# Planned decode-attention and gated-MLP backward: keys load first, layer norm by batch statistics, output weights contiguous per partition, order found anew

## The chip, the core and the metric

The kernel runs on one core of a Trainium2 chip. The metric is the device time of one execution in microseconds (us). The core has a matrix engine (TensorE, PE in the profile; its weight loads are PEld), VectorE (DVE), ScalarE (ACT), GpSimd (POOL) and SyncE (SP), which here issues transfers. Transfers between the device memory and the on-chip buffer run on 16 DMA engines.

## The reference

One step of a decoder block with its backward pass. Two rows (batch 2, one token each, 576 wide) go through a layer norm; its result feeds an attention over cached keys and values and a gated MLP without a nonlinearity, side by side:

```python
xn = _layernorm(x)                                   # (2, 1, 576), eps 1e-5
q = (xn @ wq)                                        # 32 heads of 128, 16 key heads
p = softmax(q . k * 128 ** -0.5)                     # over 4096 cached keys
a = (p @ v) @ wo                                     # wo: (4096, 576)
h = (xn @ w_gate) * (xn @ w_up)                      # 4608 wide
out = x + a + h @ w_down
```

The kernel returns `out` and the gradients, for a given `grad_out`, of x, the key and value caches, wq, wo, w_gate, w_up and w_down. All are bf16. Each cache is 33.5 MB and is read once; its gradient, of the same size, is written once. So all inputs are read and gradients of the same size are written: 92.5 MB each way.

## The kernel before

The work is cut into eight groups of two key heads (`NG`), each with two batch rows, so 16 steps (`NS`, index s; group s // 2). A step loads four 1 MB blocks (two keys, two values) into the shared buffers `big` (16 of them; `CAP`, line 298, caps how many serve as loaded blocks `kv`, transposed blocks `X`, stores being filled `st`, and gate and up blocks `G`). Per step:
- `turn` transposes each block in 32x32 tiles on DVE (L457), two instructions of 128x1024 per block.
- `softmax` and `dscore` (PE L1162) compute scores and score gradients, with small steps on DVE (L1224 the maximum, L1279, L1290) and ACT (mr, ex, pr); the results are `pp` and `dd`.
- `head_outer` (PE L1183) writes the cache gradients: the block-diagonal `BD` (built on POOL, L1150) times `pp` gives out_3 (values), times `dd` gives out_2 (keys). Each 1 MB store is evicted from PSUM in four casts of 128x1024 on ACT (L461) or DVE (L463).
- `contract` (PE L1335) gives the attention output (t = 1) and the gradient of q (t = 0), held in `oT`.

Per group, `group_front` computes q (PE L908), spreads it (`rep`, event Eq), then transposes wo (DVE L457), multiplies it with `Wdy` (PE L941) and turns the result into the second half of `qd` through `dof` (DVE L457, ACT L950); the event is Ed. `group_back` takes `oT` to `R` by PE transposes (L969) and makes out_5 (rows, casts of 128x576), out_4 (columns, casts of 128x1024; its tail in `tl`), and the sums `acc` (L987) and `accx` (L1012) for out_0 and out_1.

The MLP runs in nine blocks of 512 columns (`mlp`), loaded in pairs: gate and up (1 MB each, `G`, with their last 64 rows in `gu`) and two w_down blocks (`ww`). It writes out_8 (rows), out_6 and out_7 (columns, 1 MB per pair, complete only when both halves are done).

`front` (L564 on) loads x and grad_out by ACT's queue, computes the layer norm in five passes on ACT (L574 to L582), transposes it to `xs` (event Exn) and copies grad_out and the normed rows to all partitions (`dyr`, `xnr`, L608), and grad_out in columns to `Wdy` (event Edy). Its intermediates lie in buffers of `st`. `consts` builds selector tiles on DVE; `clears` zeroes ten tiles on POOL.

The order of everything is planned when the program is built. Each piece is a generator (a stream) that yields requests: an engine for a time, a buffer (ACQ, REL), an event (WAIT, SET), a transfer, or a priority (PRIO). `Order.run` keeps a model of each engine's and the transfer queue's time and always lets the request go on that can start first; among requests for one engine within `SLACK` of it the lowest priority number wins. Priorities come from `pr(name, s)`: a base `PR`, edges `HEAD` and `TAIL`, and an offset per step `OFF`, numbers found by a search outside the program. `EV(cols)` picks ACT or DVE for an eviction by their planned times and `BIAS`. `WQ_AT`, `WO_AT` and `MLP_AT` gate when weight loads may be issued, counted in key and value blocks already issued. What comes out is a fixed instruction order per engine; each engine runs it strictly in order. SP's order holds all loads (L1044 caches, L1059 to L1068 wq and wo, L1083 to L1092 MLP) and all stores (L681), so a store that waits for its evictions holds up every load behind it.

## Time and profile before

| | |
|---|---|
| median of 3 runs | 483.37 us (482.95 to 486.26) |
| the profiled execution, its own time | 483.47 us |
| its span, first to last instruction | 481.7 us |
| moved by DMA, mean rate | 185.94 MB, 386 GB/s |
| q1, the queue of nearly all transfers, share of 16 engines | 98.0% |
| busy: PE / DVE / ACT / POOL | 80% / 75% / 71% / 32% |
| mean granted TensorE clock | 0.675 |
| out_dram<-big stores of 1 MB | 72, 12.2 us to landing |
| key / value loads of 1 MB | 32, 11.5 us / 32, 13.1 us |
| wo loads of 576 KB | 8, 12.3 us |

The profile is one execution. Its slices give, for forty equal parts of the span, the busy tenths of each engine, the granted TensorE clock and what the DMA engines moved. A table of stretches gives the same for chosen times, with busy microseconds and counts. The DMA share is time of packets over 16 engines; packets overlap, so a full queue reads 1.00 to 1.08. The queue of an issuing engine (SPq) shows when each issue ran: an issue that waits starts late or is long, and what is merged in one line (x7) is a row of issues.

### The profile page before, as it was taken

The page shows a single profiled execution, that of the slowest core. Times are in us where ns is not written, and L with a number is a line of the kernel's source. Part 1 is how long each engine was busy: PE and PEld are TensorE (multiplying, and loading weights), DVE is VectorE, ACT ScalarE, POOL GpSimd, SP SyncE. Part 2 cuts the span into 40 slices and gives each one's busy share as a digit, 9 for nine tenths or more (in the row PEclk, how much of TensorE's full clock was granted, in tenths as well). Part 3 has the DMA queues.
Part 4 walks back from the last instruction along what each step waited for, and adds up shares of the span by engine and source line. Part 5 has one row for each costly group of instructions (what it writes and reads, how often), then busy time and mean ns, then how long its engine had stood idle before and what let it go on. Part 6 is the DMA issues. An engine that isn't in the chain of part 4 may idle for free.

```text
span 481.7 us, 15312 instructions
## 1 busy us (share of the span) xinstructions
PE 386.8 (80%) x6530; PEld 217.9 (45%) x6530; DVE 360.0 (75%) x667; ACT 343.2 (71%) x520; POOL 155.4 (32%) x220
## 2 busy tenths in 40 slices
PE   1479699858788878868977899857698899899897
PEld 1456345435444444434654345324465434554444
DVE  8688877867377977776677778866665988788872
ACT  6066578956787596755598779856578877868883
POOL 3110553443011374320026364361102724074100
PEclk9995657669656578677786557756965555765765
DMA  7997999999999999999999999999999999999994
GB/s 289 353 406 269 367 387 386 401 343 399 424 406 417 390 416 420 365 399 407 415 406 417 342 407 422 424 403 388 413 386 411 420 326 403 419 395 419 405 412 163
DMA packets 49652, 185.94 MB, mean 386 GB/s; under 512 B 4008, under 2 KB 21168, under 8 KB 33200
## 3 DMA queue, kind: packets, MB, share of 16 engines
q1 hardware_dynamic: 49576, 184.96, 98.0%
q8 instruction: 51, 0.84, 0.7%
q14 instruction: 17, 0.14, 0.1%
q10 hardware_dynamic: 8, 0.00, 0.0%
HBM read 92.48 MB, written 92.48 MB: 384 GB/s over the span
## 4 chain that ended last, share of the span: by engine, by line
DMA 46%; PE 30%; ACT 10%; DVE 7%; issue 4%; SPq 3%; DVEq 0%; ACTq 0%
DMA out_dram<-big 29%; ACT big L461 8%; PE ps_o L1183 6%; PE ps_m L1335 5%; DMA big<-in_A_k_cache_dram 5%; DMA big<-in_A_v_cache_dram 5%; PE ps_m L1162 4%; DVE big L457 3%; DMA ww<-in_B_w_down_dram 3%; PE ps_o L715 3%; DMA ww<-in_A_wo_dram 2%; PE ps_m L941 2%; DVE big L463 2%; DMA ww<-in_A_wq_dram 1%; PE ps_o L701 1%
## 5 line engine op out<-in xcount | busy, mean ns | idle before, releaser
L461 ACT CAST big<-ps_o 128x1024 bf16<-128x1024 f32 (+1 forms) x319 | 283.0, 955 | 41.0 <-PE ps_o L1183 22.1
L457 DVE STREAM_TRANSPOSE big<-big 128x1024 f32<-128x1024 f32 x146 | 175.8, 1223 | 23.9 <-DMA out_dram<-big 17.0
L1150 POOL TENSOR_TENSOR BD<-vr,mask 128x2048 bf16<-128x2048 bf16 x32 | 115.3, 3602 | 114.1 <-PE ps_o L1183 40.8
L463 DVE CAST big<-ps_o 128x1024 bf16<-128x1024 f32 (+1 forms) x57 | 66.4, 1166 | 12.8 <-PE ps_o L1183 4.3
L1162 PE MATMUL ps_m<-big,W 128*32 128x128 bf16 x2048 | 60.4, 286 | 4.2 <-POOL W L1127 1.3
L1162 PEld LDWEIGHTS <-W 128*32 128x32 bf16 x2048 | 47.8, 127 | 22.4 <-issue 19.3
L1183 PE MATMUL ps_o<-BD,dd 32*128 32x512 bf16 x256 | 51.4, 527 | 7.5 <-ACT big L461 5.5
L1183 PE MATMUL ps_o<-BD,pp 32*128 32x512 bf16 x256 | 47.6, 520 | 8.4 <-ACT big L461 6.4
L1127 POOL COPY W<-rep 32x16 bf16<-32x16 bf16 x128 | 24.5, 192 | 69.9 <-DVE rep L925 65.0
L661 POOL COPY wt<-wm 64x128 bf16<-64x128 bf16 (+1 forms) x34 | 8.9, 261 | 99.2 <-DVE wm L654 98.3
L457 DVE STREAM_TRANSPOSE big<-ww 128x1152 f32<-128x1152 f32 x25 | 34.1, 1365 | 7.5 <-DMA out_dram<-big 4.8
L1335 PE MATMUL ps_m<-big,dd 128*32 128x512 bf16 x256 | 28.8, 540 | 9.8 <-DVE dd L457 4.7
L1335 PE MATMUL ps_m<-big,pp 128*32 128x512 bf16 x256 | 30.2, 566 | 1.4 <-DVE pp L457 0.9
L1183 PEld LDWEIGHTS <-dd 32*128 32x128 bf16 x256 | 12.0, 98 | 30.6 <-issue 26.5
L1183 PEld LDWEIGHTS <-pp 32*128 32x128 bf16 x256 | 11.0, 98 | 24.7 <-issue 21.1
L701 PEld LDWEIGHTS <-xnr 32*128 32x128 bf16 x416 | 13.7, 110 | 14.4 <-issue 12.9
L715 PE MATMUL ps_o<-dyr,R 32*32 32x288 bf16 x256 | 18.1, 396 | 2.1 <-ACT big L461 1.1
L461 ACT CAST osb<-ps_m 128x512 bf16<-128x512 f32 x16 | 9.6, 598 | 12.7 <-PE ps_m L1335 9.3
L941 PE MATMUL ps_m<-big,Wdy 128*128 128x128 bf16 x144 | 15.4, 292 | 3.4 <-DVE cr L1287 1.8
L701 PE MATMUL ps_o<-hb,xnr 32*128 32x128 bf16 x288 | 14.3, 250 | 4.5 <-ACT big L461 3.2
L715 PE MATMUL ps_o<-dyr,hb 32*32 32x288 bf16 x288 | 16.1, 337 | 1.1 <-DVE tl L463 0.5
L941 PEld LDWEIGHTS <-Wdy 128*128 128x128 bf16 x144 | 13.8, 134 | 6.3 <-issue 6.3
(198 smaller groups left out, 486.6 us busy)
## 6 DMA issues: line engine op xcount, KB each, us to landing
out_dram<-big SPq DMA_DIRECT2D x72, 1024.0 KB, 12.2
big<-in_A_k_cache_dram SPq DMA_DIRECT2D x32, 1024.0 KB, 11.5
big<-in_A_v_cache_dram SPq DMA_DIRECT2D x32, 1024.0 KB, 13.1
out_dram<-big SPq DMA_DIRECT2D x17, 576.0 KB, 10.8
ww<-in_B_w_down_dram SPq DMA_DIRECT2D x9, 576.0 KB, 12.4
out_dram<-big SPq DMA_DIRECT2D x10, 512.0 KB, 9.6
ww<-in_A_wo_dram SPq DMA_DIRECT2D x8, 576.0 KB, 12.3
ww<-in_A_wq_dram SPq DMA_DIRECT2D x8, 512.0 KB, 9.7
```

Source lines behind the costliest of these rows:

```text
L457: nc.vector.transpose(out, in_)
L461: nc.scalar.copy(out, in_)
L463: nc.vector.tensor_copy(out=out, in_=in_)
L661: nc.gpsimd.tensor_copy(view(Wt[:], 64 * h, 64, 0, [[dims[-1][1], n], [1, dims[-1][1]]]), view(Wm[:], 64 * h, 64, off, dims))
L701: nc.tensor.matmul(o[:, aa, dc * P:(dc + 1) * P], lhsT=xnr[32 * a:32 * a + 32, dc * P:(dc + 1) * P], rhs=rhs(a), start=True, stop=True)
L715: nc.tensor.matmul(o[32 * q:32 * q + 32, aa, 0:HD2], lhsT=view(t, 32 * q, 32, 2 * A + aa, [[4, 32]]), rhs=dyr[32 * q:32 * q + 32, k * HD2: ...
L941: nc.tensor.matmul(dp, lhsT=Wdy[:, e, 2 * k:2 * k + P], rhs=view(X[:], 0, P, 64 * k + e, [[D, GH], [2, 32]]), start=(k == 0 and e == 0), s ...
L1127: nc.gpsimd.tensor_copy(view(W_t[t][w][:], 32 * a, 32, 6 + 8 * a, [[G * WW, 4], [WW, G], [1, 2]]), view(rep_t[grp[g]["qs"]][:], 32 * a, 32 ...
L1150: nc.gpsimd.tensor_tensor(BD_t[i][:], view(vr_t[v][:], 0, P, 0, [[0, 16], [1, Dh]]), view(mask16[:], 0, P, 0, [[1, 16], [0, Dh]]), ALU.mult)
L1162: nc.tensor.matmul(sc[32 * cq:32 * cq + 32, :], lhsT=view(W[:], 0, P, (be * G + l) * WW + 6 - 4 * c2 - 2 * l, [[1, 32]]), rhs=view(X[:], 0 ...
L1183: nc.tensor.matmul(o[:, k, :], lhsT=pr2[32 * c4:32 * c4 + 32, :], rhs=BD[32 * c4:32 * c4 + 32, 8 * l + 4 * h2:8 * l + 4 * h2 + 4, :], star ...
L1335: nc.tensor.matmul(ct[32 * j:32 * j + 32, :], lhsT=view(rT, 0, P, 4 * c + 2 * l, [[1, 32]]), rhs=kv_t[kvS[s][t][l]][:, Dh * c:Dh * (c + 4) ...
```

## The change

The layer norm takes mean and variance from VectorE's batch statistics (`bn_stats`, `bn_aggr`), then one square root on ACT and one subtract-and-multiply on DVE; ACT loads its square-root table before the rows arrive. The grad_out rows get a stream of their own (`front_y`), and the intermediates tiles of their own, so the `st` buffers are free from the start; a new event Exr stands for the normed rows on all partitions. The first key block is issued ahead of all else on SP. All clears run on DVE before the other constants. wo is loaded with four consecutive rows per partition (4608 bytes) instead of four rows 128 apart; to match, `dof` is taken through a PE transpose, and the output product reads `rT`, a transpose of `R`. A group's tail piece alternates between the halves of its buffer. The first step's key `BD` waits for Eq alone. CAP lets X hold 9 buffers instead of 12. All numbers of the search (OFF, HEAD, TAIL, PR and those shown) are new.

In the built order SP issues: the first key block, wq, wo, gate and up of the first pair with their tails, both w_down blocks, one key, two value, two key and one value block, then the first stores (out_8, two tails, out_8, out_6, out_7, two tails), then a value and a key block. Before, it was: wq, two key blocks, one value block, wo, gate and up, both w_down blocks, one value, two key and one value block, then out_8, two tails, a value and a key block, out_6, out_7. At the end, the last MLP block's loads follow the last value block; before, three key and value blocks followed them.

```diff
--- before.py
+++ after.py
-CAP = {"kv": 7, "X": 12, "st": 4, "G": 2}
...
-MLP_AT = [2.38, 3.44, 16.76, 17.06, 29.05, 44.32, 47.73, 43.88, 59.6]
-WQ_AT = [-3, 9, 17, 23, 32, 39, 50, 55]
-WO_AT = [2, 7, 5, 25, 36, 39, 37, 57]
+CAP = {"kv": 7, "X": 9, "st": 4, "G": 2}
...
+MLP_AT = [0, 6.72, 15.68, 13.64, 27.33, 41.52, 44.61, 38.32, 79.54]
+WQ_AT = [-2, 8, 17, 24, 34, 38, 50, 44]
+WO_AT = [-14, 7, 0, 22, 36, 40, 42, 56]
...
-LM, LAG = 0.15, 1.75
+LM, LAG = 0.61, 1.67
...
-BIAS = 0.547
-SLACK = {"PE": 0.08, "ACT": 0.3, "DVE": 0.46, "POOL": 24.94, "SP": 1554.58}
+BIAS = 0.347
+SLACK = {"PE": 0.04, "ACT": 0.27, "DVE": 0.49, "POOL": 11442.77, "SP": 11922.52}
...
-    dof = const.tile([P, GH, 32], FP32, name="dof")
+    dof = const.tile([P, P], BF16, name="dof")
+    rT = const.tile([P, GH, 32], BF16, name="rT")
...
-    var = const.tile([2, 1], FP32, name="var")
...
-    xs = filled("xs", [P, 6, 32], BF16, 0.0, nc.gpsimd)
-    Wdy = filled("Wdy", [P, 2, 160], BF16, 0.0, nc.gpsimd)
+    xs = filled("xs", [P, 6, 32], BF16, 0.0)
+    Wdy = filled("Wdy", [P, 2, 160], BF16, 0.0)
...
+    for t in (*W_t[0], *W_t[1], *wm_t, *wt_t, *oT_t):
+        nc.vector.memset(t[:], 0.0)
...
-    Exn, Edy, Econst, Ezero = Event(), Event(), Event(), Event()
+    Exn, Exr, Edy, Econst, Ezero = Event(), Event(), Event(), Event(), Event()
...
-        for t in (*W_t[0], *W_t[1], *wm_t, *wt_t, *oT_t):
-            yield POOL(0.37)
-            nc.gpsimd.memset(t[:], 0.0)
...
-    def carve(t, n):
-        return pairs(t[:])[0:2, D * n:D * (n + 1)]
-
...
+    xnb = const.tile([2, D], BF16, name="xnb")
+    bst = const.tile([2, 2, 6], FP32, name="bst")
+    mv = const.tile([2, 2], FP32, name="mv")
+
+    def widen(src, dst):
+        i = yield ACQ("o")
+        o = o_t[i]
+        yield PE(0.24)
+        for k in range(2):
+            nc.tensor.matmul(o[:, k, 0:HD2], lhsT=sel2[:].rearrange("b a m -> b (a m)"),
+                             rhs=src[:, k * HD2:(k + 1) * HD2], start=True, stop=True)
+        e = yield EV(D)
+        cp(e, dst[:].rearrange("p (k n) -> p k n", k=2), o[:, :, 0:HD2])
+        yield REL("o", i)
+
+    def front_y():
+        yield WAIT(Ein)
+        yield from widen(xy[:, D:2 * D], dyr)
+        dyT = xnr[:].rearrange("p (k m) -> p k m", m=32)
+        yield DVE(0.8)
+        t32(xnr[:], view(dyr[:], 0, P, 0, [[64, NB], [1, 2], [2, 32]]))
+        yield DVE(0.8)
+        for a in range(4):
+            nc.vector.tensor_copy(
+                view(Wdy[:], 32 * a, 32, 32 * a, [[2, NB], [160, 2], [1, 2]]),
+                dyT[32 * a:32 * a + 32, :, 0:2].rearrange("p (k e) b -> p k e b", e=2))
+        yield SET(Edy)
...
-        x_f, xc = carve(st_t[1], 0), carve(st_t[1], 1)
-        xnb = st_t[2][0:2, 0:D]
+        yield SPAWN(front_y(), -999.0)
+        yield ACT(1.5)
+        nc.scalar.activation(warm[:], eps_t[0:1], AF.Sqrt)
...
-        yield ACT(4.0)
-        nc.scalar.activation(x_f, xb, AF.Copy, accum_out=nmu[:])
-        nc.scalar.activation(nmu[:], nmu[:], AF.Copy, scale=-1.0 / D)
-        nc.scalar.activation(xc, x_f, AF.Identity, bias=nmu[:], scale=1.0)
-        nc.scalar.activation(x_f, xc, AF.Square, accum_out=var[:])
-        nc.scalar.activation(rstd[:], var[:], AF.Sqrt, bias=eps_t[:], scale=1.0 / D)
-        yield DVE(0.15)
+        yield DVE(1.0)
+        for k in range(2):
+            nc.vector.bn_stats(bst[:, k], xb[:, k * HD2:(k + 1) * HD2])
+        nc.vector.bn_aggr(mv[:], bst[:].rearrange("p k s -> p (k s)"))
+        yield ACT(0.3)
+        nc.scalar.activation(rstd[:], mv[:, 1:2], AF.Sqrt, bias=eps_t[:], scale=1.0)
+        yield DVE(0.6)
...
-        yield ACT(0.8)
-        nc.scalar.activation(xnb, xc, AF.Copy, scale=rstd[:])
-        yield ACT(1.7)
+        nc.vector.tensor_scalar(xnb[:], xb, mv[:, 0:1], rstd[:], op0=ALU.subtract, op1=ALU.mult)
+        yield ACT(1.5)
...
-        yield DVE(0.5)
+        yield DVE(0.4)
...
-
-        for src, dst in ((yb, dyr), (xnb, xnr)):
-            i = yield ACQ("o")
-            o = o_t[i]
-            yield PE(0.24)
-            for k in range(2):
-                nc.tensor.matmul(o[:, k, 0:HD2], lhsT=sel2[:].rearrange("b a m -> b (a m)"),
-                                 rhs=src[:, k * HD2:(k + 1) * HD2], start=True, stop=True)
-            yield DVE(0.75)
-            nc.vector.tensor_copy(dst[:].rearrange("p (k n) -> p k n", k=2), o[:, :, 0:HD2])
-            yield REL("o", i)
-            if dst is dyr:
-                dyT = st_t[3][:, 0:2 * NB * 32].rearrange("p (k m) -> p k m", m=32)
-                yield DVE(0.8)
-                t32(st_t[3][:, 0:2 * NB * 32], view(dyr[:], 0, P, 0, [[64, NB], [1, 2], [2, 32]]))
-                yield DVE(0.8)
-                for a in range(4):
-                    nc.vector.tensor_copy(
-                        view(Wdy[:], 32 * a, 32, 32 * a, [[2, NB], [160, 2], [1, 2]]),
-                        dyT[32 * a:32 * a + 32, :, 0:2].rearrange("p (k e) b -> p k e b", e=2))
-                yield SET(Edy)
-        for j in range(1, 4):
-            yield REL("st", j)
+        yield WAIT(Edy)
+        yield from widen(xnb, xnr)
+        yield SET(Exr)
...
+        nc.vector.tensor_scalar(nmu[:], mv[:, 0:1], -1.0, None, op0=ALU.mult)
...
-    def tail_outer(rhss, dsts, p, event):
+    def tail_outer(rhss, dsts, p, event, w0=0):
...
-        yield SPAWN(put(dsts, [st[64 * w:64 * w + 64, 0:FS] for w in range(nw)], 64 * FS * 2, 1024, "tl", i, done),
+        yield SPAWN(put(dsts, [st[64 * w:64 * w + 64, 0:FS] for w in range(w0, w0 + nw)], 64 * FS * 2, 1024, "tl", i, done),
...
-                for w, rhs in enumerate(rhss):
+                for w, rhs in enumerate(rhss, w0):
...
-                cp(e, st[0:64 * nw, 256 * A:256 * A + 256].rearrange("p (a f) -> p a f", a=2), o[0:64 * nw, :, 0:P])
+                r = slice(64 * w0, 64 * (w0 + nw))
+                cp(e, st[r, 256 * A:256 * A + 256].rearrange("p (a f) -> p a f", a=2), o[r, :, 0:P])
...
-        yield WAIT(Ld, Edy)
+        yield WAIT(Ld, Edy, Exr)
...
-        yield DVE(0.31)
-        t32(dof[:].rearrange("p c n -> p (c n)"), dp)
+        e = yield EV(128)
+        cp(e, view(dof[:], 0, P, 0, [[1, 4], [4, 32]]), dp.rearrange("p (c i) -> p c i", c=4))
+        yield REL("m", m)
+        m = yield ACQ("m")
+        dT = m_t[m][:].bitcast(BF16)[:, 0:P]
+        yield PE(0.0, 0.1)
+        nc.tensor.transpose(dT, dof[:], ident[:])
+        e = yield EV(8)
+        cp(e, qd[:, 1], view(dT, 0, P, 0, [[32, GH], [1, 2]]))
...
-        yield ACT(0.25)
-        nc.scalar.copy(qd[:, 1], dof[:, :, 0:2])
...
+        yield DVE(0.31)
+        t32(rT[:].rearrange("p c m -> p (c m)"), view(R[:], 0, P, 0, [[1, 4], [4, 32]]))
...
-        yield SPAWN(tail_outer([lambda a: R[32 * a:32 * a + 32, 1, :]], [out_4[512:576, n0:n0 + FS]], po, E[2]), po)
+        yield SPAWN(tail_outer([lambda a: R[32 * a:32 * a + 32, 1, :]], [out_4[512:576, n0:n0 + FS]], po, E[2], g % 2), po)
...
-                nc.tensor.matmul(yp[:, dc, :], lhsT=wo[:, h * D + DOFF[dc]:h * D + DOFF[dc] + P], rhs=oT[:, 0, h, 0:2],
+                nc.tensor.matmul(yp[:, dc, :], lhsT=wo[:, h * D + DOFF[dc]:h * D + DOFF[dc] + P], rhs=rT[:, h, 0:2],
...
-            yield PRIO(pr("load", s))
...
+                    yield PRIO(pr("load", s) if n else -1e5)
...
-                yield DMA("SP", 0.4, 128 * GH * D * 2, 1152)
-                nc.sync.dma_start(ww_t[w][:, 0:GH * D].rearrange("p (h n) -> p h n", h=GH),
-                                  A_wo[n0:n0 + FS, :].rearrange("(h p) n -> p h n", p=P))
+                yield DMA("SP", 0.36, 128 * GH * D * 2, 4608)
+                nc.sync.dma_start(ww_t[w][:, 0:GH * D].rearrange("p (c n) -> p c n", c=GH),
+                                  A_wo[n0:n0 + FS, :].rearrange("(p c) n -> p c n", c=GH))
...
-            for t in (1, 0):
+            for t in (0, 1) if s == 0 else (1, 0):
...
-                yield WAIT(grp[g]["Eq"], grp[g]["Ed"])
+                yield WAIT(*[grp[g][x] for x in (("Eq",) if s == 0 and t == 0 else ("Eq", "Ed"))])
...
-    od.used["st"] = 3
-    for j in range(1, 4):
-        od.slots["big"][j] = None
-
...
-            yield WAIT(Emore)
+            yield WAIT(Emore, Exr)
...
-        (WQ_AT[g], ("wq", g)), (WO_AT[g], ("wo", g)))]), -50.0, 1.2)
-    od.spawn(load_ws([(MLP_AT[2 * i], ("mlp", i)) for i in range((NFS + 1) // 2)]), -50.0, 1.2)
-    od.spawn(load_kv(), 0.0, 1.2)
+        (WQ_AT[g], ("wq", g)), (WO_AT[g], ("wo", g)))]), -50.0, 0.2)
+    od.spawn(load_ws([(MLP_AT[2 * i], ("mlp", i)) for i in range((NFS + 1) // 2)]), -50.0, 0.2)
+    od.spawn(load_kv(), -1e5, 0.0)
...
-    od.free["DVE"] = od.free["POOL"] = 3.0
+    od.free["DVE"], od.free["POOL"] = 2.6, 0.8
```

## The prediction

> **What bounds the kernel now.** I read the page's head and slices, then the DMA queues, then a table of stretches cut where the slices dip, the queue of SyncE (SP), which issues nearly all transfers, and the first and last microseconds engine by engine.
>
> ```profile
> span 481.7 us, 15312 instructions
> DMA  7997999999999999999999999999999999999994
> GB/s 289 353 406 269 367 387 386 401 343 399 424 406 417 390 416 420 365 399 407 415 406 417 342 407 422 424 403 388 413 386 411 420 326 403 419 395 419 405 412 163
> q1 hardware_dynamic: 49576, 184.96, 98.0%
> ```
>
> The transfers are the bound: 185 MB go through one queue that is busy 98% of the span, while PE is busy 80%, DVE 75%, ACT 71%. So only three things save time: sending no less but sooner, sending in cheaper packets, and closing holes. The table shows the holes (columns: stretch, its length, busy time and count of PE, PEld, DVE, ACT, POOL, then granted clock, DMA share, GB/s).
>
> ```profile
> 2.00:4.00 2.00, 0.00 (x0) 0.00 (x0) 2.00 (x2) 1.92 (x5) 2.00 (x9) 1.00 0.42 100
> 8.00:12.00 4.00, 1.68 (x29) 1.20 (x30) 3.10 (x7) 2.23 (x3) 0.00 (x0) 1.00 1.01 426
> 13.00:14.00 1.00, 0.00 (x0) 0.00 (x0) 0.96 (x2) 0.00 (x0) 0.00 (x0) 1.00 1.06 385
> 36.00:38.00 2.00, 1.81 (x44) 1.27 (x47) 1.99 (x5) 0.66 (x1) 0.00 (x0) 0.50 0.15 58
> 38.00:40.00 2.00, 2.00 (x46) 1.04 (x41) 2.00 (x6) 0.00 (x0) 0.00 (x0) 0.50 0.71 125
> 40.00:42.00 2.00, 1.84 (x38) 1.66 (x34) 1.94 (x5) 1.90 (x3) 0.00 (x0) 0.50 0.67 258
> 268.00:272.00 4.00, 3.50 (x20) 1.04 (x15) 3.91 (x6) 3.30 (x5) 1.29 (x1) 0.50 0.91 325
> 388.00:392.00 4.00, 4.00 (x31) 0.86 (x33) 3.39 (x5) 3.87 (x6) 0.00 (x0) 0.50 0.81 268
> 472.00:476.00 4.00, 4.00 (x54) 2.79 (x54) 1.31 (x6) 2.93 (x4) 0.00 (x0) 0.50 0.50 193
> ```
>
> See full flow at 8 to 12 (426 GB/s), and four losses: a slow start, a hole at 36 to 42, two small dips mid-way, and the tail. The queue says why:
>
> ```profile
> 0.73 1.24 SPq L1059 DMA_DIRECT2D ww<-in_A_wq_dram  x2
> 33.02 0.35 SPq L681 DMA_DIRECT2D out_dram<-big  x1
> 42.58 2.23 SPq L681 DMA_DIRECT2D out_dram<-big  x2
> 253.35 15.30 SPq L681 DMA_DIRECT2D out_dram<-big  x7
> 364.48 22.02 SPq L681 DMA_DIRECT2D out_dram<-big  x9
> 432.59 0.85 SPq L1044 DMA_DIRECT2D big<-in_A_v_cache_dram  x1
> ```
>
> The first issues are two 32 KB pieces at 0.62 us each, too small to fill the time until the third. The loads that fit the buffers (12.06 MB) are sent by about 35 us; the first large store of out_6 waits until 42.58, and the stores ahead of it carry 0.7 MB. Each dip mid-way follows a long row of stores without a load between: each waits for its evictions, and the loads sent ahead run out.
>
> **The change part by part.** The sum goes against the profiled run, 483.47 us (span 481.7 and 1.8 around it); the median of the three runs is 483.37.
>
> *Start.* A 1 MB key block goes first. From 2 to 5 us, 0.53 MB moved. The first bytes come near 2.2 us, 1.4 after the first issue; at 426 GB/s 1.19 MB would have moved by 5. The 0.66 MB short are 1.5 us; the small issues then hide behind the key block, which takes 2.5 us. I take -1.4. Ends: -1.6, and -0.5 if the first block ramps up as slowly.
>
> *Output weights.* Eight loads of 0.59 MB go from packets of 1152 B to 4608 B. The microsecond 13 to 14 is nearly all 1152-byte packets: 385 GB/s at full share; 8 KB packets make 426. 4608 B lies nearer to the latter, say 420: 1.53 - 1.40 = 0.13 us each, -1.0. Ends: 0 and, if such packets shared with others lose twice as much, -2.0. The Trainium skill ("DMA: Bandwidth & Descriptors", Specifications) puts the least transfer for line rate at 512 B, by which 1152-byte rows would already run full and the sum would be 480.2 instead of 479.2. The trace is against that: 385 at full share, not 426.
>
> *First hole.* The built order sends, after one key block: wq, wo, gate and up, both w_down blocks, and only then six key and value blocks. So the second w_down has 5.77 MB up to its end instead of 7.87: 2.1 MB, 5 us, with the start 6.4 us sooner. It landed at 27.4 (the DVE transpose of it starts 27.41), so about 21 after. DVE then runs in order: w_down transpose 1.37, half of the second key block 1.22, two L826-like products 0.4 each, four small transposes 0.3 to 0.4, the other half 1.22; out_8's first store goes at about 27.5, not 33.0. ACT then has, up to out_6's store, six casts of 1.0, six of 0.65 and 1.3 of small ones (tl, and mr and ex of the softmax): 11.2 us from about 25.5, so out_6 near 37; pr and two more casts (2.4), out_7 near 39.6. The loads run dry at 32.6, the first out_8 and the tl stores cover to 34.4, the second out_8 store issues at 35 and flows at 36.5: a hole of about 2.1, and 0.4 ahead of out_6. Now the hole costs (2.52 MB possible less 0.88 moved from 36 to 42) / 426 = 3.9 us. I take 2.5 left, -1.4. Ends: -3.9, and +1 if these casts run behind a PE at clock 0.5 from 28 on instead of 36. The price: scores of step 0 come at 28 to 30 (DVE L1224 at 23.8 before), as the second key block is now behind the weights; out_3's first store was only at 58, so it has the slack.
>
> *Layer norm, streams, clears.* ACT gives up about 3.3 us of passes and one of three 1.28 us table loads. DVE gains bn_stats, a 2x576 pass and 12 clears (near 0.15 each by its own accx clear of 0.19), and loses the wait beside POOL: its two selector copies took 3.12 and 3.48 us while POOL cleared, four copies of that size 0.49 in all later. DVE is in order: bn_stats stand behind the first key transpose, which waits for landing near 6; xs comes at about 12, as before (11.5). The new waits for Exr stop mlp and the group backs, which come at 18 and later; xnr is cast near 11. Twelve clears leave POOL, whose next work is a copy of W at 18.7. Cover: the gate weights, which land only at 16. Cost 0; without that cover 0.5.
>
> *Groups.* Per group: DVE L457 dof 0.32 and ACT 0.20 become an eviction of 128 (0.28), a PE transpose (0.1) and an eviction of 8 (0.15); rT adds a transpose of 0.3. Eight times some 0.4 us on DVE or ACT. Cover: DVE idles 25%. The event Ed comes about 0.4 us later and nothing at the bound waits for it in time; the tail pieces only change halves of their buffer. 0, up to +1.
>
> *Middle.* I counted the bytes in unbroken rows of stores in both orders. Before, ahead of the last: 9.1, 8.2 and 6.0 MB the longest; the dips at 384 to 400, 264 to 276 and 164 to 168 stand at the ends of just these; a row of 5.4 MB (from 334) left no dip. After: none above 5.4 MB. The dips' missing share is 0.28 + 1.0 + 1.24 = 2.5 us; the tighter X cap of 9 keeps fewer blocks transposed ahead. I take -2.0. Ends: -3 and +3, since a new order can wait elsewhere.
>
> *Tail.* The last MLP block's loads now follow the last value block (before, three key and value blocks followed them). Behind that value block stand 15.3 MB, not 12.4: at 410 GB/s it lands 7.2 us sooner against the end. But its MLP work then lies behind it too. By the row durations, from mr of step 15 (447.1) to R of the last group (465.8), the new order holds 23.5 us of ACT work and 22.1 of DVE work, where the trace has 15.9 and 14.8. ACT at nine tenths busy (its 31.8 of 36 us from 432 on) takes 26.1, DVE at eight tenths (29.0 of 36) 27.6, against 17.4 from the landing at 448.4 to R: 10.2 more, 3.0 net of the 7.2. From R to the end it stays 15.9 us, the same chain. Between 0, if the engines fill their gaps, and 3.0 I take the middle, +1.5; ends -1 and +5.
>
> Sum: 483.47 - 1.4 - 1.0 - 1.4 - 2.0 + 1.5 = 479.2 us.
>
> **The rivals.**
> *All holes close, no tail price:* -1.4 - 3.9 - 1.0 - 2.5 = 474.7. For it: DVE is busy only 1.6 of the 4 us from 22 to 26, so the first hole's chain can be run sooner. Against: ACT's eight casts before out_7 need 8 us anyway. 0.23.
> *Hidden anyway:* early bytes only make the loads run dry sooner, as buffers cap them and the evictions set the first stores; the middle keeps its dips elsewhere. Only wo is gained: 482.5. For it: the same 12.06 MB before the first store. Against: the stores' own input comes 6 us sooner. 0.17.
> *Slower, the tail decides:* landing of the last value block + 27.6 + 15.9 + 1.8 is the time. By my terms it lands at 448.4 - 7.2 - 5.8 = 435.4. It becomes slower than before from a landing after 438.2, by 1% after 443; at 445, if the block waits for its buffer, 490. For it: ACT and DVE are 0.9 and 0.8 busy from 432 on, so work put there shows. Against: nothing shows that block waiting more than 0.85 us at issue (432.59). 0.18.
> *The change does not do what it says:* the built order does have keys first and 4608-byte wo rows, so no.
>
> **How the numbers follow.** The forecast holds 0.42, its own range 476 to 482, and three sevenths of it lie below 478.6. A measurement here can tell about 1% (4.8 us) from no change. Faster: 0.23 + 0.18 = 0.41. Slower by over 1%: 0.14 of the tail case's 0.18. Within: 0.45. The range leaves out a tenth on each side: from 474.5, where all holes close, to 487, a landing at 441.7 in the tail case.
>
> **What would show it.** DMA share near 1 already from 2.5 us; out_8's first store at 27 to 28, out_6's at 36 to 38; 58 GB/s nowhere for two whole microseconds; no dip below 0.9 between 60 and 430; the last value block landing near 435 and R 25 to 28 us later. Wrong if out_6's store stays at 42, if new dips appear, or if the share falls before 455.

## The result, and the profile after

The changed kernel takes 485.7 us (median of 20 runs, 483.72 to 488.45), the kernel before 482.65 us (20 runs, 481.38 to 486.26): the ratio is 1.0059, 95% interval 1.0040 to 1.0077. Two later measurements of the same program (a_x12 and a_same below) gave 1.0103 (1.0069 to 1.0138) and 1.0071 (1.0047 to 1.0095). So the change made the kernel slower by some 0.6 to 1%, about 3 to 5 us, where 4.3 us less were forecast. The profiled execution of the changed kernel took 484.28 us, span 482.4. It is faster than the median of its program, and the profiled execution of the kernel before (483.47 us, span 481.7) is slower than the median of its own, so the two traces differ by 0.7 us of span, and not by 3.0 as the medians do.

Its page shows the same bytes and the same full queue:

```profile
span 482.4 us, 15326 instructions
DMA  8999999999999999999999999999899999999995
GB/s 292 382 408 356 391 419 381 339 364 406 415 394 410 361 424 377 381 415 419 374 381 408 408 423 427 342 414 415 309 380 370 416 344 422 424 421 372 424 397 210
q1 hardware_dynamic: 46504, 184.96, 98.2%
```

The start and the first hole are better, as was forecast (GB/s 289 to 292 in the first slice, 269 to 356 in the fourth), and the last slice is fuller (163 to 210). But there are new low slices: 339 at 84 to 97 us, 309 at 338 to 350. The table of stretches (stretch, length, busy time and count of PE, PEld, DVE, ACT, POOL, granted clock, DMA share, GB/s) shows what stood behind them:

```profile
2.00:4.00 2.00, 0.00 (x0) 0.10 (x1) 1.97 (x15) 1.05 (x2) 0.00 (x0) 1.00 0.72 266
36.00:38.00 2.00, 2.00 (x46) 1.37 (x43) 1.42 (x3) 2.00 (x4) 0.00 (x0) 0.50 0.85 335
38.00:40.00 2.00, 1.68 (x44) 1.29 (x48) 1.97 (x5) 1.15 (x4) 0.70 (x1) 0.50 1.02 382
84.00:88.00 4.00, 3.70 (x76) 1.97 (x77) 4.00 (x6) 4.00 (x5) 0.70 (x1) 0.50 0.71 283
268.00:272.00 4.00, 3.43 (x74) 1.94 (x72) 3.81 (x9) 2.69 (x4) 2.14 (x5) 0.50 1.02 412
320.00:328.00 8.00, 6.40 (x70) 4.56 (x67) 3.51 (x6) 0.86 (x2) 7.11 (x4) 0.57 1.02 423
344.00:348.00 4.00, 3.46 (x62) 2.06 (x59) 4.00 (x6) 4.00 (x9) 0.00 (x0) 0.50 0.86 310
388.00:392.00 4.00, 4.00 (x63) 1.94 (x59) 3.19 (x8) 2.56 (x4) 1.82 (x9) 0.50 0.88 299
472.00:476.00 4.00, 3.63 (x70) 2.25 (x58) 1.49 (x7) 3.30 (x6) 0.00 (x0) 0.75 0.76 296
```

The hole at 36 to 40 and the dip at 268 are gone, the dip at 388 is smaller. At 84 to 88 and 344 to 348 the queue is short of work while DVE and ACT are both busy 4.00 of 4 us; at 320 to 328 ACT had only 0.86 of 8. SP's queue names the issues around these places:

```profile
28.20 0.35 SPq L687 DMA_DIRECT2D out_dram<-big  x1
34.50 4.34 SPq L687 DMA_DIRECT2D out_dram<-big  x3
...
73.37 5.05 SPq L687 DMA_DIRECT2D out_dram<-big  x3
78.52 0.68 SPq L687 DMA_DIRECT2D out_dram<-tl  x1
83.81 3.99 SPq L687 DMA_DIRECT2D out_dram<-big  x2
87.89 0.37 SPq L1058 DMA_DIRECT2D big<-in_A_v_cache_dram  x1
...
330.21 0.34 SPq L1058 DMA_DIRECT2D big<-in_A_k_cache_dram  x1
330.65 2.69 SPq L687 DMA_DIRECT2D out_dram<-tl  x2
335.31 0.34 SPq L687 DMA_DIRECT2D out_dram<-big  x1
336.95 1.91 SPq L687 DMA_DIRECT2D out_dram<-tl  x2
341.26 0.34 SPq L687 DMA_DIRECT2D out_dram<-big  x1
343.86 0.34 SPq L1058 DMA_DIRECT2D big<-in_A_v_cache_dram  x1
346.29 1.15 SPq L1073 DMA_DIRECT2D ww<-in_A_wq_dram  x2
...
388.65 0.34 SPq L1058 DMA_DIRECT2D big<-in_A_v_cache_dram  x1
...
427.78 0.33 SPq L1058 DMA_DIRECT2D big<-in_A_v_cache_dram  x1
```

From 78.52 to 83.81 nothing is issued, then stores that wait for their casts; from 330.65 to 343.86 only 1.4 MB go out (four stores of 64 KB, two of 0.59 MB).

To say where the time went, slow packets and dry stretches must be put on one scale. I count each packet of the trace at the median time of its size (8192 B 309 ns, 4608 B 178, 2048 B 84, 1152 B 51, 1024 B 46, 512 B 27, 4 B 9) over 16 engines: 450.8 us of work before, 449.1 after. The loss of a stretch is its length less the work that its packets make; the losses and the work add up to the span.

| loss, us | before | before again (b_x9) | after | after again (a_same) | after again (a_x12) |
|---|---|---|---|---|---|
| 0 to 32 | 4.7 | 4.5 | 4.0 | 3.6 | 4.5 |
| 32 to 52, the first hole | 4.6 | 4.4 | 2.0 | 3.3 | 2.9 |
| 52 to 76 | 2.6 | 2.6 | 0.6 | 0.5 | 0.1 |
| 76 to 96 | 0.7 | 0.3 | 3.2 | 3.5 | 3.8 |
| 96 to 334 | 6.9 | 8.0 | 9.7 | 9.3 | 9.2 |
| 334 to 368 | 1.1 | 0.4 | 4.7 | 4.6 | 4.3 |
| 368 to 440 | 3.0 | 3.3 | 2.5 | 2.2 | 3.3 |
| 440 to the end | 7.2 | 6.6 | 6.6 | 6.4 | 8.3 |
| sum | 30.9 | 30.2 | 33.3 | 33.4 | 36.4 |
| span | 481.7 | 480.9 | 482.4 | 482.6 | 485.6 |

b_x9 and a_x12 (below) turned out to have the orders of before and of after. Executions of one order differ by up to 1.3 us in the first hole, 1.1 at 96 to 334 and 1.9 at the end, so only larger differences can be read there. Those at 52 to 76, 76 to 96 and 334 to 368 stand in every pair.

At 76 us the changed kernel had 7.0 us less work left than the kernel before; at 358 us it was level, at 384 it was 2.6 us behind.

### The profile page after: what moved, and what is told of

The parts are those of the page before. It is cut to its first block, busy times and chain, and to the rows that moved or that the text cites. A ratio compares the mean times of both kernels' runs of the same rounds, so it can differ in the third digit from the quotient of the medians.

```text
span 482.4 us, 15326 instructions
## 1 busy us (share of the span) xinstructions
PE 380.2 (79%) x6538; PEld 219.1 (45%) x6538; DVE 362.0 (75%) x692; ACT 339.4 (70%) x513; POOL 152.2 (32%) x208
## 5 line engine op out<-in xcount | busy, mean ns | idle before, releaser
L464 ACT CAST big<-ps_o 128x1024 bf16<-128x1024 f32 (+1 forms) x314 | 281.0, 957 | 50.0 <-PE ps_o L1197 33.4
L466 DVE CAST big<-ps_o 128x1024 bf16<-128x1024 f32 (+1 forms) x62 | 69.4, 1121 | 13.1 <-PE ps_o L1197 5.4
L1176 PEld LDWEIGHTS <-W 128*32 128x32 bf16 x2048 | 46.7, 124 | 24.5 <-issue 22.7
L1197 PE MATMUL ps_o<-BD,dd 32*128 32x512 bf16 x256 | 49.6, 531 | 9.5 <-ACT big L464 7.3
L1349 PE MATMUL ps_m<-big,dd 128*32 128x512 bf16 x256 | 27.8, 526 | 0.9 <-DVE oT L1369 0.4
L674 PE MATMUL ps_m<-big,wm 128*32 128x128 bf16 x416 | 13.4, 290 | 7.0 <-DVE hb L814 3.0
L464 ACT CAST tl<-ps_o 128x256 bf16<-128x256 f32 (+1 forms) x22 | 7.4, 371 | 15.2 <-PE ps_o L777 15.1
L948 PE MATMUL ps_m<-big,Wdy 128*128 128x128 bf16 x144 | 16.0, 297 | 2.2 <-DVE big L460 2.2
L721 PE MATMUL ps_o<-dyr,hb 32*32 32x288 bf16 x288 | 15.9, 345 | 2.3 <-ACT big L464 1.3
L707 PE MATMUL ps_o<-hb,xnr 32*128 32x128 bf16 x288 | 15.3, 270 | 2.8 <-ACT big L464 2.2
L827 PE MATMUL ps_m<-big,Wdy 128*128 128x128 bf16 x162 | 15.8, 276 | 2.1 <-DVE hb L833 1.0
(201 smaller groups left out, 485.7 us busy)
```

The lines of the kernel that those rows point to most:

```text
L464: nc.scalar.copy(out, in_)
L466: nc.vector.tensor_copy(out=out, in_=in_)
L707: nc.tensor.matmul(o[:, aa, dc * P:(dc + 1) * P], lhsT=xnr[32 * a:32 * a + 32, dc * P:(dc + 1) * P], rhs=rhs(a), start=True, stop=True)
L721: nc.tensor.matmul(o[32 * q:32 * q + 32, aa, 0:HD2], lhsT=view(t, 32 * q, 32, 2 * A + aa, [[4, 32]]), rhs=dyr[32 * q:32 * q + 32, k * HD2: ...
L827: nc.tensor.matmul(dh, lhsT=Wdy[:, e, 2 * k:2 * k + P], rhs=view(X[:], 0, P, 64 * k + e, [[D, FC], [2, 32]]), start=(k == 0 and e == 0), s ...
L948: nc.tensor.matmul(dp, lhsT=Wdy[:, e, 2 * k:2 * k + P], rhs=view(X[:], 0, P, 64 * k + e, [[D, GH], [2, 32]]), start=(k == 0 and e == 0), s ...
```

## The experiments

The measure is the ratio to the kernel before, measured beside each. As the three measurements of one and the same changed program differ by 0.4%, times of different groups are not compared to less than that; the stretches of the traces are.

**One part alone.** *b_wo* and *a_wo* change only how the output weights are read, in either direction:

```diff
-  ww_t[w][:, 0:GH * D].rearrange("p (h n) -> p h n", h=GH), A_wo[n0:n0 + FS, :].rearrange("(h p) n -> p h n", p=P)
+  ww_t[w][:, 0:GH * D].rearrange("p (c n) -> p c n", c=GH), A_wo[n0:n0 + FS, :].rearrange("(p c) n -> p c n", c=GH)
```

> The kernel before, its order of instructions untouched on every engine; only the eight output-weight loads are read as 4608 contiguous bytes per partition, which mixes up the weight's rows, so out and what hangs on it are not the reference's. Packet theory (the prediction's wo term, -1.0 us): the trace of before has 4096 packets of 1152 B at a median of 51 ns, the new ones are 1024 at 178 ns, over 16 engines 13.1 against 11.4 us; the time falls by 1.0 to 1.7 us, ratio 0.9965 to 0.998. Contention theory: in the changed kernel the packets of 4608 B averaged 196.6 ns and those of 8192 B 321.8 (before 191.4 and 320.0), so what the shorter rows cost is paid in slower long packets; ratio 0.999 to 1.002 and q1's packet time within 0.5 us of 471.9.

Measured: 0.9983 (0.9961 to 1.0005), q1's packet time 469.0 us against 472.0.

> The changed kernel, its order untouched; only the eight output-weight loads are read in the old rows of 1152 B, so out is not the reference's. Packet theory: 1.0 to 1.7 us slower than the changed kernel (ratio to before about 1.008 to 1.0095, where the changed kernel has 1.0059). Contention theory: no difference, ratio 1.005 to 1.007.

Measured: 1.0070 (1.0046 to 1.0094), packet time 475.3 against 473.8. Both have the sign that the packet theory gives, but neither is clear of the error (0.8 us with an interval that holds 0, and nothing to 0.5), and the packet time of the same packets is 471.0 us in b_x9 and 474.0 in b_key. So the gain of the longer rows is not shown in the time.

*b_key* issues the first key block ahead of all else:

```diff
+    nc.sync.dma_start(kv_t[0][:], views[0][0, 0])
     od.run()
...
-                    nc.sync.dma_start(kv_t[i][:], views[t][b, G * g + l])
+                    if n == 0:
+                        assert i == 0, i
+                    else:
+                        nc.sync.dma_start(kv_t[i][:], views[t][b, G * g + l])
```

> The kernel before, with one move in SP's queue: the first key block is issued ahead of the first group's query weights, into the same buffer; the order of all else, and all other engines, as before. If the start term holds (-1.4 us) the bytes moved by 4 us rise from 0.20 to about 0.65 MB and the time falls by about 1.0 to 1.4 us, ratio 0.997 to 0.998. If an early lead only makes the loads run dry sooner, the hole at 36 to 42 us grows by the same and the ratio is 0.999 to 1.001.

Measured: 0.9986 (0.9960 to 1.0011). The first 8 us lose 2.9 us instead of 3.6 (3.5 in b_x9). What becomes of this lead cannot be read from one execution: at 184 us b_key has 0.8 us less work left than before, but b_x9, with nothing moved, has 0.9 less; by 280 b_key is level.

*b_best* puts both parts into the order of before, with what the new rows need (L950 and the output product):

```diff
-        t32(dof[:].rearrange("p c n -> p (c n)"), dp)
+        cp("DVE", view(dof[:], 0, P, 0, [[1, 4], [4, 32]]), dp.rearrange("p (c i) -> p c i", c=4))
+        dT = m_t[m][:].bitcast(BF16)[:, 512:512 + P]
+        nc.tensor.transpose(dT, dof[:], ident[:])
+        cp("ACT", qd[:, 1], view(dT, 0, P, 0, [[32, GH], [1, 2]]))
...
+        t32(rT[:].rearrange("p c m -> p (c m)"), view(R[:], 0, P, 0, [[1, 4], [4, 32]]))
...
-  rhs=oT[:, 0, h, 0:2]
+  rhs=rT[:, h, 0:2]
```

> The kernel before, with the order of its plan kept and two parts of the change put into it by hand: the first key block is issued ahead of the weights, and the output weights are read as 4608 B per partition, with what this needs (an eviction of dp, a transpose on PE and a copy per group in the place of the transpose and copy on DVE and ACT, and a transpose of R on DVE). The parts-add theory: 0.7 us (measured for the key block alone) and 0.8 us (for the rows alone) add up, the additions are hidden; the time falls by 1.0 to 2.0 us, ratio 0.996 to 0.998. Additions-cost theory (the structure itself costs on DVE, ACT and PE, 8 groups of some 0.4 us): ratio 1.000 to 1.004. If the order is all that counts and early bytes are lost again later: 0.999 to 1.001.

Measured: 1.0000 (0.9976 to 1.0024). The parts do not add up to the gain that was hoped for, though the interval only just excludes it. At 96 us it is 2.5 us ahead of before, at 384 still 1.9, at 404 0.8, at 468 0.5 behind. Where the lead goes is in the last group; that the added transposes and evictions cost it is not ruled out by the time.

**The numbers of the plan.** All numbers from CAP to PR exchanged between the two kernels (a_oldnum, b_newnum), or the one cap (a_x12, b_x9):

```diff
-CAP = {"kv": 7, "X": 9, "st": 4, "G": 2}
+CAP = {"kv": 7, "X": 12, "st": 4, "G": 2}
```

> The changed kernel's structure (keys first, batch statistics, stream of its own, contiguous output weights, new tail halves) under all of before's planner numbers: OFF, HEAD, TAIL, PR, gates, CAP with X 12, BIAS, SLACK, LM, LAG. Structure-gains theory (start, first hole and wo together -3.8, the new numbers give it back in the middle): not slower than before, ratio 0.990 to 0.998. Structure-costs theory (the added transposes and evictions, the rearranged groups cost 3 us): 1.004 to 1.010, as the changed kernel. Fit theory (planner numbers fit one structure; any other gives an order with more holes): 1.010 to 1.040, with the DMA share below 0.9 in more stretches than either kernel.

Measured: 1.0633 (1.0589 to 1.0676).

> The structure of before under all of the changed kernel's planner numbers. Structure-gains theory: slower than the changed kernel by what the structure gains, ratio 1.012 to 1.016. Structure-costs theory: not slower than the changed kernel, ratio 1.000 to 1.005. Fit theory: slower than both, 1.010 to 1.040, with holes at other places than either.

Measured: 1.0574 (1.0528 to 1.0619). Both are far slower than either kernel, and slower than any of the theories said. The DMA slices, a_oldnum first:

```profile
DMA  8987999999999759999999989999999899998665
```

```profile
DMA  7999399999999939999999998799999999899994
```

The fit theory has the kind, and its range (up to 1.040) was too small: the numbers fit one structure, and numbers that do not fit cost 28 to 31 us, ten times what any part of the change is worth.

> The changed kernel with the cap of the transposed blocks X at 12, as before, instead of 9; all other numbers as in the changed kernel. If the tight cap makes the new holes (loads have no buffer because too few blocks may be transposed ahead), the holes at 80 to 92 and 340 to 352 close and the ratio is 0.997 to 1.002. If 9 never binds, nothing changes: 1.004 to 1.008. If the numbers were fitted to the cap, the order is another one with holes elsewhere: 1.008 to 1.030.

Measured: 1.0103 (1.0069 to 1.0138). The order came out the same on every engine: a cap of 9 never binds here, and this is the changed kernel once more.

> The kernel before with the cap of transposed blocks X at 9 instead of 12, all else as before. If the plan of before never holds more than 9, the order is the same and the ratio 0.999 to 1.001. Fit theory (any one number changes the order all through): the order differs on every engine and the time rises by 0.5 to 3%, ratio 1.005 to 1.030. If a tighter cap by itself costs stretches of dry queue: the same rise, with new stretches of DMA share below 0.9 at places where before had none.

Measured: 0.9990 (0.9969 to 1.0011), again with the order of before untouched. The prediction's remark that the tighter cap keeps fewer blocks ahead was empty in both.

**The new gaps.** *a_ahead* moves loads ahead of waiting stores, in SP's queue alone:

```diff
+    HOLD, FLUSH = {179, 180, 181, 182, 183, 46}, {187, 47}
+    held, nsp = [], [0]
+
+    def sp(d, x):
+        k, nsp[0] = nsp[0], nsp[0] + 1
+        if k in HOLD:
+            held.append((d, x))
+        else:
+            nc.sync.dma_start(d, x)
+        if k in FLUSH:
+            for y in held:
+                nc.sync.dma_start(*y)
+            held.clear()
...
-            nc.sync.dma_start(d, x)
+            sp(d, x)
```

> The changed kernel, all engines but SP untouched; in SP's queue two moves: the value block issued at 87.89 goes ahead of the store that waited at 83 to 87 us for its evictions (its buffer was free from about 83.9), and the group's query and output weights issued at 346.3 to 348.6 go ahead of the stores and the value block issued at 335.3 to 343.9. Queue theory (loads that could go stand behind stores that wait): the DMA share of 84 to 92 rises from 0.83 to above 0.9 and that of 340 to 352 from 0.84 to above 0.95, and the time falls by 1.0 to 2.5 us against the changed kernel, ratio to before 1.0005 to 1.004. Buffer theory (the loads had nowhere to go): the moved loads wait at the queue's head and hold the stores up; no gain, ratio 1.005 to 1.009.

Measured: 1.0065 (1.0041 to 1.0090); the share of 84 to 92 stayed 0.83, that of 340 to 352 fell to 0.81. The moved weights waited at 336 to 342 for landings and held up the stores. The queue theory, as I had it, falls: order on SP alone does not close the gaps.

*a_half* halves evictions:

```diff
+    HALF = {"ACT": {*range(33, 48), *range(207, 220)}, "DVE": {38, 39}}
+    nbig = {"ACT": 0, "DVE": 0}
+
     def cp(e, out, in_):
+        if out.tensor.name.startswith("big") and in_.tensor.name.startswith("ps_o"):
+            if nbig[e] in HALF[e]:
+                h = out.shape[-1] // 2
+                out, in_ = (x[(slice(None),) * (len(x.shape) - 1) + (slice(0, h),)] for x in (out, in_))
+            nbig[e] += 1
```

> The changed kernel with work left out: of the evictions from PSUM into the large store buffers, the 30 that ran at 76 to 92 and 336 to 352 us copy only the first half of their columns (so parts of out_2 to out_8 are not the reference's); order, matmuls and transfers are untouched. ACT was busy 4.00 of 4 us from 84 to 88 and from 344 to 348, DVE 4.00 too, while in the stretches without a hole ACT had 0.9 of 8 us (320 to 328). Eviction theory (at the new holes ACT and DVE are the bound, since the order brings the evictions in bunches): the DMA share of 84 to 92 rises from 0.83 to above 0.95 and that of 340 to 352 from 0.84 to above 0.95; the two holes miss 3.7 us, so the time falls by 2 to 3.5 us, ratio to before 0.998 to 1.002. Rival (PE at half clock or the landings set the holes): the evictions only idle longer, both shares stay below 0.9, ratio 1.004 to 1.008.

Measured: 1.0041 (1.0013 to 1.0069). Its stretches:

```profile
84.00:88.00 4.00, 3.46 (x62) 1.93 (x64) 3.92 (x7) 3.73 (x8) 0.00 (x0) 0.50 0.94 354
344.00:348.00 4.00, 3.89 (x78) 2.61 (x70) 4.00 (x8) 3.05 (x9) 0.00 (x0) 0.50 0.74 252
```

The first gap closes (the loss of 76 to 96 falls from 3.2 to 1.5). In part this is because the queue is 3.1 us behind when it comes there, but the row itself is shorter too: from its first store (73.37 in the changed kernel) to the value block (87.89) it takes 13.1 us, where the changed kernel takes 14.5 and a_same and a_x12 15.0. So there the evictions are a bound. The second gap does not close (334 to 358 loses 3.4, after 2.9): the theory is right for one gap and wrong for the other. The execution traced, 488.59 us, is the slowest of its ten; by the medians of its group a_half (484.09) is 3.1 us faster than a_x12 (487.17), which is the changed kernel, so the time gives the eviction theory more than this trace does, and where the remainder of it was gained is open. What SP waited for in the second, in the changed kernel (total, times, longest):

```profile
SPq L687 <- DMA out_dram<-big: 4.5, 3, 2.3
SPq L1058 <- DMA out_dram<-big: 4.1, 2, 2.2
SPq L687 <- DMA big<-in_A_v_cache_dram: 2.5, 2, 1.9
SPq L687 <- ACT big L464: 2.5, 4, 1.4
SPq L1073 <- DMA big<-in_A_k_cache_dram: 2.1, 1, 2.1
```

Landings, not casts. The last line tells the rule: the query weights go into `ww` and need no key block; the key block of 330.21 is the transfer eight places before them. In this program each issue waits for the landing of the eighth before it: of the 122 issues of this trace whose eighth predecessor has a recorded landing, none ended before it, while of 123 with the seventh 39 did. So eight are in flight, and here four of the eight (K, two small, one large, two small, one large, V) were stores of 64 KB. *a_lane* issues the weights first and these four small stores later; *a_notl* is the same without them:

```diff
+    AFTER = {187: [179, 182, 183], 190: [177, 178, 180, 181]}       # a_lane
+    AFTER = {187: [179, 182, 183], 100000: [177, 178, 180, 181]}    # a_notl
+    HOLD = {k for ks in AFTER.values() for k in ks}
+    held, nsp = {}, [0]
+
+    def sp(d, x):
+        k, nsp[0] = nsp[0], nsp[0] + 1
+        if k in HOLD:
+            held[k] = (d, x)
+        else:
+            nc.sync.dma_start(d, x)
+        for j in AFTER.get(k, ()):
+            nc.sync.dma_start(*held.pop(j))
...
-            nc.sync.dma_start(d, x)
+            sp(d, x)
```

> The changed kernel, all engines but SP untouched, no byte left out; in SP's queue the group's query and output weights (issued at 346.3 to 348.6) go ahead of the two out_8 stores and the value block (335.3, 341.3, 343.9), and the four 64 KB stores of 331 to 339 go behind the next group's query weights. Eight-in-flight theory (each issue waits for the landing of the transfer eight places before it; SP's waits of 330 to 354 are 16 us of landings against 11 of evictions; from 330.7 to 343.8 the issues carried 1.4 MB): without the small stores between, the weights go at 332 to 336 instead of 346, the DMA share of 340 to 352 rises from 0.84 to above 0.95, and the time falls by 1.0 to 2.0 us against the changed kernel, ratio to before 1.002 to 1.004. Buffer theory (the weights' buffers are free only at about 345, as their old content is still in use, or the stores' evictions set the flow): the weights wait at the queue's head; share below 0.88, ratio 1.005 to 1.009.

Measured: 1.0041 (1.0014 to 1.0067).

```profile
344.00:348.00 4.00, 3.52 (x78) 2.42 (x71) 3.96 (x6) 4.00 (x9) 0.00 (x0) 0.50 1.00 367
352.00:356.00 4.00, 3.43 (x68) 1.48 (x61) 2.60 (x4) 1.58 (x2) 0.00 (x0) 0.60 0.58 189
```

The gap at 340 to 352 is gone (share 0.98), and a deeper one stands where the small stores now are (issued 350.1 to 354.8). The time cannot be told from that of the changed kernel.

*a_same* is the changed kernel, unedited, in the group of the next three:

> The changed kernel itself, once more, as the reference of this call. It measured 1.0059 (1.0040 to 1.0077) at first, and 1.0103 (1.0069 to 1.0138) as a_x12, which turned out to have the same order on every engine: between 1.004 and 1.010.

Measured: 1.0071 (1.0047 to 1.0095).

> As a_lane (the query and output weights ahead of the out_8 stores and the value block), but the four 64 KB stores of 331 to 339 us are left out, so four tail pieces of out_6 and out_7 are missing (0.26 MB, 0.6 us at 410 GB/s). Eight-in-flight theory: no gap is left between 334 and 358, the share stays above 0.95, the loss of this stretch falls from 2.9 us (a_lane 4.5) to below 1.5; the time is 1.5 to 3 us below the changed kernel, ratio 0.4 to 0.6% below that of a_same. Buffer theory (the gap follows from late evictions, whatever is in flight): a gap of 1.5 us or more remains between 340 and 358; at most 0.2% below a_same.

Measured: 1.0044 (1.0029 to 1.0058), 0.27% below a_same.

```profile
344.00:348.00 4.00, 3.80 (x72) 2.60 (x67) 4.00 (x6) 4.00 (x8) 0.00 (x0) 0.50 0.98 368
348.00:352.00 4.00, 3.40 (x36) 1.33 (x39) 2.77 (x7) 2.96 (x4) 0.00 (x0) 0.50 0.80 285
352.00:356.00 4.00, 3.08 (x52) 0.90 (x42) 3.13 (x4) 2.40 (x4) 0.56 (x1) 0.50 1.06 399
384.00:388.00 4.00, 3.21 (x31) 0.93 (x28) 3.96 (x8) 4.00 (x7) 1.09 (x1) 0.67 0.59 215
```

Between a_lane and a_notl only four stores of 64 KB differ: the loss of 334 to 358 is 4.5 against 1.2 us, for 0.26 MB. That is the size the eight-in-flight theory gave, though a dip to 0.80 is left at 348 to 352. The time lies between what the two theories said: of a lead of 4.0 us over a_same at 384 us only 0.27% (1.3 us) reached the end. A longer gap stands at 384 to 388, where ACT and DVE are busy 4.00 and 3.96.

*a_tlpool* and *b_tlpool* send the small stores through GpSimd's queue:

```diff
-            nc.sync.dma_start(d, x)
+            (nc.gpsimd if tag == "tl" else nc.sync).dma_start(d, x)
```

> The changed kernel, its order kept; the 26 small stores of 64 KB go through GpSimd's queue instead of SP's, so that they neither hold SP up while their evictions run nor take one of the eight places. Eight-in-flight theory: the gap of 340 to 352 (share 0.84) rises above 0.9, SP's waits for landings of 30.5 us (stores) and 31.4 us (loads) fall; ratio 0.2 to 0.6% below a_same. Rival: GpSimd, in order, now waits for these evictions, and the block-diagonal products behind them (3.6 us each) come late; the time rises, ratio 0.2 to 1.0% above a_same.

Measured: 1.0057 (1.0036 to 1.0078).

> The kernel before with the same one edit: its 26 small stores through GpSimd's queue. Before has no gap at 334 to 358, and its SP queue waits 16.4 us for evictions of the small stores; eight-in-flight theory: it gains less than the changed kernel does, ratio 0.996 to 1.000. Rival (GpSimd held up): 1.002 to 1.010.

Measured: 1.0018 (0.9999 to 1.0036). Neither theory is borne out in size. In a_tlpool the share of 344 to 348 is 0.70: one of the large stores there waits 7.0 us for its cast on DVE, then the value block 3.4 us for the landing of the store that empties its buffer, and the weights stand behind both. So the second gap needs both to go, the small stores and the order of weights behind the value block: a_ahead moved the weights alone and a_tlpool the small stores alone, and the gap stayed; a_lane and a_notl moved both, and it went.

**Where a lead ends.** The value block after the row of stores near 390 is issued at 388.65 in the changed kernel (above). In a_notl, which is 3.0 us of work ahead of it at 384 us, and in before:

```profile
387.91 0.34 SPq L413 DMA_DIRECT2D big<-in_A_v_cache_dram  x1
```

```profile
389.94 0.34 SPq L1044 DMA_DIRECT2D big<-in_A_v_cache_dram  x1
```

3.0 us of lead bring 0.7; in b_best, 1.9 us ahead of before, it is issued at 389.50, 0.4 sooner. In these traces the block waits last for the landing of the store that empties its buffer, and the traces of the changed kernel and of a_notl show what sets that: the store goes out when its cast on ACT ends, at 377.2 in the changed kernel and at 378.7 in a_notl, so the lead made the cast no sooner. Only the landing was quicker, 9.2 us instead of 11.4. So a lead turns into a longer gap (384 to 404 loses 2.1 us in the changed kernel and 4.4 in a_notl; 2.9 in before and 4.1 in b_best). A lag does carry over: a_lane, 3.9 us behind the changed kernel at 384, issues the block at 391.64. No version tried is faster than the kernel before by more than its interval.

## Why the prediction was wrong, step by step

*Bound.* "The transfers are the bound", from which the prediction had that only three things save time, was the wrong premise: true of the share of the span (98%), not of each place. Where the stores wait for casts (near 83 and near 377) the engines set the time, and most of a lead is lost there.

*Start,* -1.4: right in kind, 0.7 to 0.8 us in the first 8 us (3.57 to 2.81; b_key 3.57 to 2.90); the forecast was twice that.

*Output weights,* -1.0: by packets 4096 x 51 ns / 16 = 13.1 us become 1024 x 178 / 16 = 11.4, -1.7; by the time 0.8 us with an interval that includes 0. The rule weighed in the prediction, full line rate from 512 B on (the Trainium skill, "DMA: Bandwidth & Descriptors", Specifications), does not agree with the packets of these traces: 512 B in 27 ns are 19 GB/s per engine, 1152 B 23, 4608 B 26, 8192 B 27.

*First hole,* -1.4: out_8's store went at 28.20 (forecast 27 to 28), out_6's in the row from 34.50 to 38.84 (36 to 38). The loss fell by 2.6 us in the execution shown; in the eight other executions of the changed kernel and its variants it fell by 0.3 to 2.4 (3.3 in a_same, so 1.3).

*Middle,* -2.0, ends -3 and +3: this is the step that failed. "I counted the bytes in unbroken rows of stores": the rows became shorter, the old dips at 264 to 276 went (-1.7 us) and 384 to 404 shrank, as said, but the losses from 52 to 440 us rose from 14.3 to 20.6, +6.3 (a_same +5.8), past the upper end (a_x12 against b_x9: 14.6 to 20.7). The length of a row does not tell where a gap comes. New gaps stand behind rows of 4.3 MB (73 to 88) and 1.4 MB (330 to 344): the first because 15 casts of 1.0 us came due on ACT in 16 us, the second because eight transfers in flight held four small ones and the value block waited for its buffer. "No dip below 0.9" met 0.71, 0.78, 0.86, 0.87 and 0.88. About 1.7 us of the +6.3 I can place in the first gap's evictions (a_half, with the reserve made there), 3.4 in the second with what follows it (a_notl: 334 to 368 lose 1.4 instead of 4.7). What is left is +2.8 at 96 to 334 (+1.3 in a_x12 against b_x9) and 1.0 in the two gaps, less 2.1 at 52 to 76 and 0.5 at 368 to 440. At 96 to 334 the changed kernel loses most at 184 to 200 (2.1), 228 to 252 (1.8) and 304 to 316 (2.0). These are not gaps. After, then before:

```profile
308.00:312.00 4.00, 3.90 (x88) 2.40 (x90) 3.78 (x7) 3.31 (x5) 3.12 (x1) 0.50 1.05 308
```

```profile
308.00:312.00 4.00, 3.44 (x116) 1.93 (x108) 4.00 (x7) 3.13 (x6) 1.86 (x1) 0.99 1.02 420
```

The queue is full, and the packets are slow: while weights in packets of 2 KB run there (half of the bytes at 304 to 316), these take 108 ns on average where the median of the whole trace is 84, and those of 8192 B 340 ns where it is 309. The kernel before shows the same at 200 to 228 (2048 B at 109 ns, a loss of 1.4 us). For 52 to 440 us as a whole the time that the packets took tells the two apart: of the +6.3 us, 3.5 are a queue that is short of packets, 2.8 are slower packets. No run tested what makes the packets slow.

*Tail,* +1.5: -0.7 (7.2 to 6.6) in the executions shown, but +1.7 in a_x12 against b_x9 (6.6 to 8.3), so its sign is not settled. The working was off in each part: the last value block landed at 442.1, not 435, since the middle had eaten the lead; R stood 23.1 us later in the execution shown, not 25 to 28 (25.6 in a_x12), with ACT busy 20.4 us of them and DVE 19.9, where the working had counted 23.5 and 22.1; and from R to the end it took 17.2 us (16.8 in a_same and in a_x12), not the 15.9 of before (16.7 in b_x9).

*The sum.* Between the two executions shown the losses give -0.7 up to 32 us, -2.6 in the first hole, +6.3 in the middle and -0.6 at the end, the lighter packets -1.7: together the 0.7 us between the spans. Between b_x9 and a_x12 it is +0.1, -1.5, +6.1, +1.7 and -1.7, together 4.7.

*Layer norm, clears, groups,* 0: nothing in the traces speaks against it; not measured alone.

Of the rivals, "hidden anyway" had the mechanism (early bytes run dry elsewhere); its price was too low, as it let the middle stay as it was. "The tail decides" came out slower too, but not by its own working: from the landing at 442.1 it would give 487.4 us, and this execution took 484.28.

## What to carry to other kernels

A queue that is 98% busy is not the bound everywhere: look at each place where it runs short, and ask what time the next wait there would end if the queue came sooner; a lead is worth only what passes the next engine-set wait. Count transfers in flight, not bytes alone: four small ones in a window of eight cost 3.3 us here. Trace the same program more than once before a difference of 1 or 2 us in one stretch is read. When an order is searched anew, judge it by the places where evictions bunch up and not by the parts of the change, as the order outweighs them.

## What the runs showed of the hardware

PE's granted clock fell to 0.50 at about 34 us and was there in most stretches in which PE was busy (36 to 38: busy 2.00 of 2.00 at 0.50; of the 52 stretches of 4 us with PE busy for over 3.5, 34 were granted at most 0.55). The Trainium skill ("TensorE: Matmul & The Clock Gate", Part 1) says the opposite for the gate that it describes, that sustained activity releases the clock; this trace does not agree. Executions of the changed program differ in when it fell: with 1.00 at 28 to 32 us (after, a_wo) the stretch 32 to 52 lost 2.0 and 2.2 us, with 0.74 and 0.50 (a_same, a_ahead) 3.3 and 3.3. But a_notl, with 1.00, lost 2.9, and a_x12, with 0.67, lost 2.9 as well. So the tie between the clock and the first hole is loose, and the clock was not varied by itself.

The packet time of the same 185 MB varied by execution, 472.0 us before and 474.0 in b_key, with the same packets; gains of 1 us in packets cannot be seen in one profile.
